# The first batch in halves: q over all partitions in natural head order, swapped weight rows, g on GpSimd's queue, and a new order of the work

## The chip, the cores and the metric

One Trainium2 chip, one of its cores. The time of a kernel is the device time of one execution in microseconds (us). TensorE (PE) multiplies matrices, VectorE (DVE), ScalarE (ACT) and GpSimd (POOL) work on elements, SyncE (SP) starts most transfers. The engines run each its own list of instructions in order and wait for each other through semaphores.

## The reference

Inputs are q, k and v of shape 8 x 8 x 576 x 64 (batch, head, token, element), a vector g of 64, and the weights of four experts.

```python
kv = np.einsum('bhsd,bhse->bhde', k, v)
out = np.einsum('bhsd,bhde->bhse', q, kv)
rms = np.sqrt(np.mean(out * out, axis=-1, keepdims=True) + 1e-06)
x = out / rms * g_norm          # then x as batch x token x 512
...
logits = x @ w_gate             # the two best of four experts, with softmax weights w
for e in range(E):
    q, k, v = x @ wq[e], x @ wk[e], x @ wv[e]
    scores = scale * (q @ k.transpose(0, 2, 1))   # causal
    a = softmax(scores)
    ye = a @ v @ wo[e]
    out += (w where e was chosen) * ye
```

So there are two stages: linear attention without a mask over eight heads with a norm on each head's 64 elements, and a mixture of four causal attention experts with heads of 64 elements.

## The kernel before

All sizes are fixed: eight batches, 576 tokens, which are five blocks of up to 128 (`NB`), and 512 elements, which are four chunks of 128 (`NCH`, two heads each). The work is written as some 1,100 small tasks, each a function in the table `emit`: for example `("kv", b, c)` is the product of k and v of chunk c of batch b. The string `ORDER` lists all tasks by number, `ENGINE` gives each task its engine (S is SP's queue, C ACT's queue, A ACT, V DVE, G POOL), and `SLOTS` gives the buffers and the PSUM banks. The loop at the end issues the tasks in the listed order, so that each engine's own order and each DMA queue's order are written out by hand.

A batch goes through these tasks. `lk` and `lv` load k and v, each in four transfers (four heads by one part of the tokens) that write every second partition. `lq` loads q: the even chunks in one transfer over 128 partitions, the odd chunks in two transfers over 64 neighbouring partitions each, because in odd chunks the two heads stand in swapped order (`head`, line 307). `kv` makes the products in PSUM (line 389), `kvc` copies them to `kvs` and `kvx` moves blocks of 32 partitions to `kvm` (lines 394 to 404). `qc` turns q by 32 x 32 blocks on DVE (line 411). `o` multiplies q with `kvs` and `kvm` (line 424; one task for each pair u of chunks), `oc` copies the result to `ob`, `sq` squares it to `sqs`. `ms` sums the squares of each head by matmuls (line 456). `ln`, `rs`, `na`, `nb` and `lo` make the reciprocal root with one Newton step (lines 472 to 492), on 128 partitions for the whole batch. `bc` spreads the root over a head's elements (line 531) and `xm` multiplies it with `ob` into `xT` (line 538). `G`, `R`, `L` and `lt` make the gate logits in the same way. Then come the projections `qp`, `kp` and `v` (lines 610 and 590), the scores `sc`, `exp` and `msk`, the products `pv`, the turned result `ot`, the output products `y`, and the stores `st`.

The vector g is folded into the weights: `lw` loads a weight matrix in two halves, and `ws` scales its rows by g while it copies them (line 367); `wgs` does this for the gate's weights (line 352). `lgv` and `lwg` load g and the gate's weights on ACT's queue.

`ZEROS` puts matmuls of zeros ahead of some tasks, 61 in all, whose results nobody reads. Each matmul on 32-bit data appears as two passes in the profile.

Loads on SP's queue share eight completion semaphores in turn: a load waits until the one eight places before it has landed.

Of the kernel before, what the change touches and what calls it, by code (L numbers as in the profile page):

```python
# [10 lines left out]
FP32 = mybir.dt.float32  # L11
# [21 lines left out]
    "1d4j6Y3T1V6S3N6W4f1c3S1Z1I1g4h3U4k3Z1-6X1J3O4d4eAX3V3a204i1x4g0P6U2+1D6P1y3W1E3J4l1F3K213g4p1f2-4m6Q6R3X8T4n1e"
    "4r4t1t1h1u3Y6i6T6k3o1i1z3L304s6l4q4o3q3p1j3M1+1k6V224u3r3d4v3b3w6j233c2425398b8Y3fAc4x3s4y3y4z4+3A6Z6a3t6b8c6c"
    "3z4-3x551l6d506h593C8W6g3u566f5B4w0RAa8U3v5A6e1m8Z573h5C518V586m3B6o6n266q6u3P6s3H8X3Q5V0Q5R6r8a6t5X6p5S3D5W5L"
    "8m523I6v8o426w6y3E536x8d6zCY8e415M3e278f6+6-8g5470AbCd5YEb3F76715Z0S778h7C2H3G7D5a3i2E8l8p5u8j2IAd3j8i3kAW725s"
    "3l8n5D7A7B5N5v2FEi78AU5P5t5Q798k5OCZ8r5b8w8yEh5c5d8q5G3-3+5e8s3m738x5f5+8u5g5j7460Cc61405y3n5w758tAn66435-7t44"
    "5xAV7Y8z7uAo457Q7R5lAY5EAq5FAZ65645z7W7S7E8v7Z5T5U8+Ae5H5I90Af9146927X7TAg93Ec94Ah7gAi7e9GCf7hEe9AAp47Ak7O7f9H"
    "2BCh7vAj487P5J2C7w637a9E95Cg9B9C8-5kAlAm4I5i5K7b9D9FEa4J5h5mAsAx4L7F5n5o5pEf964M7x7zEZ62AzAy7k7yCuArAtAv499a9S"
    "A+9b7UAw9Q67Au7+A-9T7H9R689769866A7G98CbB07cB1B25qB37V7m9928CrCsB44A7d7I7j84297M2DB56B7l4F9I4G7N7i9L6C9z4K7J9+"  # L40
    "5r9cBDCt9x9Y4H9dBHBE9J9y9kB6Ca9Z7-B7BI9l9iBB809j9K7K7nBCCe7L9-A37oCiCjCkClEdB87pA481A0CmBF7qCnB9BG8283CqCp9eA1"
    "Co9fA24C4D6D6ECwCvCxD1CyC-D2CzEtEgEjEkElEmD09gA5C+9hEsD387857r8889A9D5D68AEvA6En6M8BEoEq7sBbD7BZ6J6NBc9UBd9MD8"
    "EuByBA9N9WEr6FBeD9BJ6K9nBz9mDAB+9pEpBT9XBR9VBUBfBa9O9q9oB-BSBK4BDJA8DHD4BgDKDFDIDLBlDB8CBm6GDGDMEwBr6H8DEyExEz"
    "E+9PA7Bh9rBLF0BMF29sAABi8NBVF3F18OC2BWBqC0E-9tC3DCF4C6ABC19uC4DD2JCBBjC7ACC5AD8KDhDEBkF6AEBXDNBNAFF7DfF88LBYAG"
    "9vBn8QDi9w8RF9FADgFIFJF5AHDj2GBoFGDnDoFBBOFCFD8H4NFHC8DODZ8EDaDkE0BPBpFE8FFKCCE1FL2ABQAIALDVFMAJAM6IDWFFFNDrE2"
    "DQFiE3FOBs8MFjDpDP8IDRFPCAC9BtDqBuDlDmBvE4CDE5CEFRCFBwCGBxFQDtFgFhDSFc8JEADuEBDvE8E6FdE9EFFSFmE7AODbDcFnARDXDT"
    "DYAPFTANG9G7GAFaAS6OG8DsDdFbCHFoFUGBDeFqCIFrDwDUECFpCSCMEGEEAKEDDxGCFYFWCNDyGFDzFVCTFkFXGD6LFwFuGJFZEHGGEIGLGE"
# [3 lines left out]
ENGINE = (
    "SSSSSSSSSSCCVSVSASASASGSVSASAVVVVVVGGVVVVVVVAAAAAAVAVVAAAVVGVVVVVVVVVVVVVGAVGVVGVVVAVVVVVAVVVAVAVAVAVAGGGGGVVG"
    "VVAVVVAVAVAVAVAGGGGGVVGVVAVASVASVASVASSSSSSSSSSSVVVVAVVGAVVVVVVAAVAAGAGVVAAAVVGVVVGVVVVVVVVVGAGGVVGVVVVVAVAVAV"
    "VVAVAVAVAVAGGGGGVVGVVVVAVAVAVAVAVAGGGGGVVGVVVVASVVSVASVASVASSSSSSSSSSSVVVVVGGGGVVVVVVVGAGAAAGVVAAAVVVVVVVVVVVV"
    "VVVVGAGGVVGVAVAVVVAVAVVVAVAVAVAVAGGGGGVVGVVAVAVAVAVAVAVAGGGGGVVGVVAVVSVASVASVASSSSSSSSSSSVVVVAVVGGVVVVVVAGVAAA"
    "VGVVAAAVVVVVVVVVFVFVVVVGAGGVVGVVVAVVVAVVVVVAVAVAVAVAGGGGGVVGVVAVAVAVAVAVAVAGGGGGVVGVVVVVSVASVASVVSVASSSSSSSSSS"
    "SVVVVAGGGAVVVVVVVGAGAGVGVVAAAVVGVVVGVVVVVVVVVGAGGVVGVAVVVAVVVAVVVAVAVAVAVAGGGGGVVGVVAVAVVVAVAVAVAGGGGGVVGVVVVA"
    "SVASVASVASSSSSSSSSSSVVVVAGGVAVVVVVVVAAAAGVGVVAAAVVGVVVVVVFVVVFVVGAGGVVGVVVVVVVAVAVVVAVAVAVAVAGGGGGVVGVVVVAVAVA"
    "VAVAVAGGGGGVVGVVVVASVASVVSVASVASSSSSSSSSSSVVVVAAVGGVVVVVVVAVGAAAGVVAAAVVGVVVVVVVVVVVVVGAVGVVGVVVVVVVAVAVVVAVAV"
    "AVAVAGGGGGVVGVVVVAVAVAVAVAVAGGGGGVVGVVAVASVASVASVASSSSSSSSSSSVVVVVGGGAVVVVVVAGAAVAAGVVAAAVVGVVVVVVFVFVFVVGAGGV"  # L60
    "VGVVVAVAVVVVVAVVVAVAVAVAGGGGGVVGVVVGVVVVAVVVVVAVAVAVAGGGGGVVGVVVGVVAVAVASVVSVASVASVAS"
)
# [14 lines left out]

def names(nb):
# [36 lines left out]
def kernel(  # L115
# [232 lines left out]

    def lwg():
        queue(("lwg",)).dma_start(wg_in[:], moe_w_gate.rearrange("(n p) e -> p n e", p=P))  # L350
# [481 lines left out]
```

## Time and profile before

| | |
|---|---|
| median of 3 runs | 210.72 us (209.38 to 211.36) |
| the profiled execution | 210.22 us, of which the span from the first to the last instruction is 208.5 us |
| mean granted TensorE clock | 0.993 |
| busy, share of the span | PE 94%, PEld 78%, DVE 59%, ACT 62%, POOL 35% |
| moved by DMA | 40.33 MB, mean 193 GB/s |

PE is the matmul, PEld the load of its weights, which overlaps it. A row of the timeline gives the start in us, the length in us, the engine, the line of the kernel, the operation, what it writes and reads, the count, and in brackets the idle time before it and what ended that. A row of the chain of work gives start, length and what the end of the program waited for at that time. SPq and ACTq are the issue of transfers on the queue of SP and ACT.

### The profile page before, as it was taken

To read this page: it belongs to the slowest core of one execution; us is meant where nothing else is said; L and a number is where in the kernel's file an instruction comes from. 1 tells how busy PE (TensorE), PEld (TensorE's weight loads), DVE (VectorE), ACT (ScalarE), POOL (GpSimd) and SP (SyncE) were. 2 spreads that over 40 slices of the span, in tenths; PEclk is the share of its full clock that TensorE was granted. 3 is DMA by queue.
4 is the path that set the end of the run, shared out by engine and by line. 5 is a ranking of instruction groups with operands and counts; after the bars stand their busy time and mean duration, and the time that the engine had idled before them with its cause. 6 is when DMAs were issued, how large, how long until landed. Compare 5 with 4: busy or idle time off the path is not lost.

```text
span 208.5 us, 7342 instructions
## 1 busy us (share of the span) xinstructions
PE 195.4 (94%) x3066; PEld 163.2 (78%) x3066; DVE 123.3 (59%) x305; ACT 129.6 (62%) x229; POOL 73.7 (35%) x185
## 2 busy tenths in 40 slices
PE   7779879999999999999999999999999999999990
PEld 7768556688988687869886879888976969898970
DVE  7007449457874954977576497474686566734550
ACT  2000722765986765667576677868549955688881
POOL 6001013510793260429162343234707331532510
PEclk9999999999999999999999999999999999999997
DMA  4999995999999993879259806144001010814685
GB/s 111 302 290 284 360 218 143 302 267 217 332 357 348 248 319 140 206 197 371 79 145 252 288 3 202 65 174 135 0 13 43 9 46 0 293 62 183 233 304 195
DMA packets 34385, 40.33 MB, mean 193 GB/s; under 512 B 9008, under 2 KB 25392, under 8 KB 34352
## 3 DMA queue, kind: packets, MB, share of 16 engines
q1 hardware_dynamic: 33520, 39.56, 63.4%
q8 instruction: 24, 0.39, 0.8%
q10 hardware_dynamic: 832, 0.30, 0.7%
q14 instruction: 9, 0.07, 0.1%
HBM read 30.42 MB, written 9.44 MB: 191 GB/s over the span
## 4 chain that ended last, share of the span: by engine, by line
PE 83%; DMA 8%; ACT 4%; DVE 2%; issue 1%; SPq 0%; POOL 0%; ACTq 0%; DVEq 0%; POOLq 0%
PE banks L610 17%; PE banks L590 9%; PE banks L389 9%; PE banks L424 8%; PE banks L640 8%; PE banks L456 8%; PE banks L685 7%; PE banks L758 6%; PE banks L793 3%; PE banks L531 3%; DMA v_b<-in_v_dram 3%; DMA k_b<-in_k_dram 3%; PE banks L728 2%; DMA out_dram<-stage 2%; ACT stage L301 1%; PE banks L514 1%
## 5 line engine op out<-in xcount | busy, mean ns | idle before, releaser
L652 ACT ACTIVATE PT<-banks 128x1024 bf16<-128x1024 f32 (+1 forms) x64 | 51.0, 838 | 11.8 <-PE banks L640 10.4
L659 POOL TENSOR_SCALAR_AFFINE_SELECT PT<-PT 128x256 bf16<-128x256 bf16 (+1 forms) x80 | 29.4, 386 | 15.3 <-ACT PT L652 14.7
L538 DVE TENSOR_TENSOR xT<-banks,ob 128x576 fp32r<-128x576 f32 x32 | 23.5, 748 | 5.6 <-PE banks L531 4.8
L411 DVE STREAM_TRANSPOSE qT<-q_b 128x576 f32<-128x576 f32 x32 | 23.4, 754 | 4.0 <-DMA q_b<-in_q_dram 4.0
L448 POOL TENSOR_TENSOR sqs<-ob 128x576 f32<-128x576 f32 x17 | 19.4, 1146 | 16.0 <-ACT ob L301 15.4
L590 PE MATMUL banks<-wv_r,xT 128*128 128x256 f32 x160 | 24.8, 286 | 0.1
L389 PEld LDWEIGHTS banks<-v_b,k_b 128*64 128x64 f32 x640 | 19.6, 138 | 5.5 <-DMA v_b<-in_v_dram 2.2
L389 PE MATMUL banks<-v_b,k_b 128*64 128x64 f32 x640 | 21.1, 224 | 2.9 <-DMA v_b<-in_v_dram 2.9
L640 PE MATMUL banks<-qTp,kT 64*128 64x192 f32 (+3 forms) x224 | 22.4, 308 | 0.3 <-issue 0.3
L590 PEld LDWEIGHTS banks<-wv_r,xT 128*128 128x128 f32 x160 | 21.1, 189 | 1.1 <-issue 0.5
L640 PEld LDWEIGHTS banks<-qTp,kT 64*128 64x128 f32 x224 | 16.2, 185 | 6.1 <-issue 2.2
L758 PE MATMUL banks<-wo_b,OT 128*128 128x256 bf16 x144 | 20.4, 274 | 0.0
L610 PE MATMUL banks<-xT,wq_r 128*128 128x288 f32 x128 | 20.3, 300 | 0.0
L424 PE MATMUL banks<-qT,kvs 32*64 32x288 f32 x256 | 19.6, 411 | 0.4 <-DVE xT L538 0.3
L793 PE MATMUL banks<-zeros 128*128 128x128 f32 x122 | 16.4, 296 | 3.8 <-DVE root L484 1.2
L610 PE MATMUL banks<-xT,wk_r 128*128 128x288 f32 x128 | 19.7, 298 | 0.0
L793 PEld LDWEIGHTS banks<-zeros 128*128 128x128 f32 x122 | 15.4, 208 | 5.0 <-DVE root L484 1.7
L301 ACT COPY stage<-banks 128x512 f32<-128x512 f32 x30 | 17.2, 594 | 2.9 <-PE banks L758 1.7
L424 PE MATMUL banks<-qT,kvm 32*64 32x288 f32 x256 | 18.2, 411 | 0.3 <-DVE kvm L302 0.3
L402 POOL COPY kvm<-kvs 32x256 f32<-32x256 f32 x19 | 7.6, 398 | 29.8 <-ACT kvs L301 16.2
L301 ACT COPY ob<-banks 128x576 f32<-128x576 f32 x20 | 12.3, 646 | 9.0 <-PE banks L424 9.0
L610 PEld LDWEIGHTS banks<-xT,wq_r 128*128 128x128 f32 x128 | 17.7, 188 | 0.3 <-issue 0.2
(93 smaller groups left out, 312.0 us busy)
## 6 DMA issues: line engine op xcount, KB each, us to landing
out_dram<-stage SPq DMA_DIRECT2D x32, 256.0 KB, 2.9
k_b<-in_k_dram SPq DMA_DIRECT2D x16, 320.0 KB, 6.9
v_b<-in_v_dram SPq DMA_DIRECT2D x16, 320.0 KB, 6.9
q_b<-in_q_dram SPq DMA_DIRECT2D x8, 576.0 KB, 8.2
q_b<-in_q_dram SPq DMA_DIRECT2D x15, 288.0 KB, 7.9
k_b<-in_k_dram SPq DMA_DIRECT2D x16, 256.0 KB, 5.9
v_b<-in_v_dram SPq DMA_DIRECT2D x16, 256.0 KB, 6.0
out_dram<-stage SPq DMA_DIRECT2D x8, 128.0 KB, 2.8
```

Source lines behind the costliest of these rows:

```text
L301: return nc.scalar.copy(dst, src)
L389: use(nc.tensor.matmul(p_kv[hh * Dh : (hh + 1) * Dh, c, :], lhsT=k_t(b)[:, h, j, :], rhs=v_t(b)[:, h, j, :], start=(j == 0), stop=(j == LO ...
L411: nc.vector.transpose(q_part(b, dh)[:, ms].rearrange("p m (t i) -> p m t i", t=RUN), q_t(b)[:, ms, :, dh * 32 : (dh + 1) * 32],)
L424: use(nc.tensor.matmul(bank(n)[at : at + Dh, 0:HALF], lhsT=(kvs if z == dh else kvm)[b % 2][pp, m], rhs=q_part(b, dh)[pp, m], start=(dh == ...
L538: use(nc.vector.tensor_tensor(out=at_half(xTs[b % 2], u, z), in0=both(ns)[:, :, 0:HALF], in1=ob[:, u::2, z * HALF : (z + 1) * HALF], op=Al ...
L590: use(nc.tensor.matmul(bank(n)[:, 0 : E * Hd], lhsT=blocks_of(xTs[b % 2], c)[:, i * P : (i + 1) * P], rhs=w_r["v"][:, c, :, :].rearrange(" ...
L610: use(nc.tensor.matmul(bank(ns[s])[:, 0:HALF], lhsT=w_r[nm][:, c, 2 * pr : 2 * pr + 2, :].rearrange("p e f -> p (e f)"), rhs=blocks_of(xTs ...
L640: use(nc.tensor.matmul(bank(ns[el])[:, o : o + hi - lo], lhsT=kTs[(2 * b + pr) % 3][pp, kb * P : (kb + 1) * P], rhs=tiles["qTp", b, pr][pp ...
L652: use(nc.scalar.activation(PTs[(2 * b + pr) % 3][:, :, 512 * j : 512 * j + o], both(ns)[:, :, 0:o], ACTF.Exp, scale=scale), *ns)
L659: nc.gpsimd.affine_select(out=d, in_=d, compare_op=AluOpType.is_ge, fill=0.0, base=0, pattern=[[0, 2], [1, w]], channel_multiplier=-1,)
L758: use(nc.tensor.matmul(bank(n)[:, cols], lhsT=OT[:, pr, at : at + P], rhs=wo_b[:, pr, cols], start=(pr == 0), stop=(pr == EP - 1), skip_gr ...
L793: use(nc.tensor.matmul(bank(at)[:, 2 * P : 3 * P], lhsT=zeros[:, 0:P], rhs=zeros[:], start=True, stop=True, skip_group_check=True), at)
```

## The change

The heads stand in natural order in every chunk, so that one load brings a pair of chunks over all 128 partitions. Odd chunks of `xT` now hold their two heads the other way round than before, which the weights make up for: `ws` swaps the two groups of 64 rows of odd chunks while it scales, in three instructions instead of one, and `wgs` does the same. g and the gate's weights are loaded by GpSimd's queue. Batch 0 goes in two halves (chunks 0 and 1, chunks 2 and 3) from `kv` to `xT`: each half has its own PSUM bank, its own copies and moves, its own sums, and its own root on 64 partitions. `ZEROS` holds 48 matmuls instead of 61. `ORDER`, `ENGINE` and `SLOTS` are new for the whole program; batch 0 now starts with heads 4 to 7.

```diff
 ZEROS = {
-    ("kv", 0, 0): 28, ("kv", 0, 2): 4, ("o", 0, 1): 17, ("ms", 0): 6, ("bc", 0, 0, 0): 6,
+    ("kv", 0, 2): 31, ("kv", 0, 0): 14, ("o", 0, 0): 3,
 }
...
+def halves_of(b):
+    return ((0,), (1,)) if b == 0 else ((),)
...
     def head(hh, c):
-        return 2 * c + (hh ^ (c % 2))
+        return 2 * c + hh
...
-    def lq(b, odd):
-        eng = nc.scalar if b == 0 else nc.sync
-        if not odd:
-            nc.sync.dma_start(
-                q_t(b)[:, ::2].rearrange("i m t d -> i m (t d)"),
-                q[b].rearrange("(m k a) (i t) d -> k (a i) m (t d)", k=2, a=2, t=RUN)[0],
-            )
-            return
-        for a in range(2):
-            (eng if a else nc.sync).dma_start(
-                q_t(b)[a * Dh : (a + 1) * Dh, 1::2].rearrange("i m t d -> i m (t d)"),
-                q[b, head(a, 1) :: 4].rearrange("m (i t) d -> i m (t d)", t=RUN),
-            )
+    def lq(b, u):
+        nc.sync.dma_start(
+            q_t(b)[:, 2 * u : 2 * u + 2].rearrange("i m t d -> i m (t d)"),
+            q[b, 4 * u : 4 * u + 4].rearrange("(m a) (i t) d -> (a i) m (t d)", a=2, t=RUN),
+        )
 
     def lgv():
         for h in range(2):
-            queue(("lgv",)).dma_start(g_part[h * Dh : (h + 1) * Dh], g_norm.unsqueeze(1))
+            nc.gpsimd.dma_start(g_part[h * Dh : (h + 1) * Dh], g_norm.unsqueeze(1))
 
     def lwg():
-        queue(("lwg",)).dma_start(wg_in[:], moe_w_gate.rearrange("(n p) e -> p n e", p=P))
+        nc.gpsimd.dma_start(wg_in[:], moe_w_gate.rearrange("(n p) e -> p n e", p=P))
+
+    def parts():
+        yield slice(0, P), slice(0, P), 0
+        for h in range(2):
+            yield slice(h * Dh, (h + 1) * Dh), slice((1 - h) * Dh, (2 - h) * Dh), 1
...
     def ws(nm, p):
...
-        if engine["ws", nm, p] == "A":
-            nc.scalar.mul(out, src, g_part[:, 0:1])
-        else:
-            ew(("ws", nm, p)).tensor_scalar_mul(out=out, in0=src, scalar1=g_part[:, 0:1])
+        for to, pp, odd in parts():
+            d, x, g = out[to, :, odd::2], src[pp, :, odd::2], g_part[pp, 0:1]
+            if engine["ws", nm, p] == "A":
+                nc.scalar.mul(d, x, g)
+            else:
+                ew(("ws", nm, p)).tensor_scalar_mul(out=d, in0=x, scalar1=g)
...
+    def kv_bank(b, c):
+        return small("kv", b, c // 2) if b == 0 else small("kv", b)
+
+    def chunks(h):
+        return slice(2 * h[0], 2 * h[0] + 2) if h else slice(0, NCH)
+
+    def rows_of(h):
+        return slice(h[0] * Dh, (h[0] + 1) * Dh) if h else slice(0, P)
...
-    def kv_copy(b):
-        (n,) = small("kv", b)
-        use(copy(("kvc", b), kvs[b % 2][:].rearrange("p c d -> p (c d)"), bank(n)[:, 0 : NCH * Dh]), n)
+    def kv_copy(b, *h):
+        (n,) = kv_bank(b, chunks(h).start)
+        p_kv = bank(n)[:, 0 : NCH * Dh].rearrange("p (c d) -> p c d", c=NCH)
+        use(copy(("kvc", b) + h, kvs[b % 2][:, chunks(h)], p_kv[:, chunks(h)]), n)
...
-    def ln(b):
-        ms, n = part_sums(b)
-        use(nc.scalar.activation(root[:], ms, ACTF.Ln, bias=eps[:, 0:1], scale=1.0 / Dh), n)
+    def ln(b, *h):
+        ms, n = part_sums(b, h)
+        pp = rows_of(h)
+        use(nc.scalar.activation(root[pp], ms, ACTF.Ln, bias=eps[pp, 0:1], scale=1.0 / Dh), n)
...
     def xm(b, u, z):
         ns = big("bc", b, u, z)
+        cs, cols = slice(2 * u, 2 * u + 2) if b == 0 else slice(u, NCH, 2), slice(z * HALF, (z + 1) * HALF)
         use(nc.vector.tensor_tensor(
-            out=at_half(xTs[b % 2], u, z), in0=both(ns)[:, :, 0:HALF], in1=ob[:, u::2, z * HALF : (z + 1) * HALF],
-            op=AluOpType.mult,
+            out=xTs[b % 2][:, 0 : NCH * S].rearrange("p (n s) -> p n s", s=S)[:, cs, cols],
+            in0=both(ns)[:, :, 0:HALF], in1=ob[:, cs, cols], op=AluOpType.mult,
         ), *ns)
```

The start of the new order, as the engines' lists have it (later tasks are left out):

```
SP    lk 0 heads 4-7 part 0, lv 4-7 part 1, lk 4-7 part 1, lv 0-3 part 1, lv 4-7 part 0, lk 0-3 part 0,
      lq 0 chunks 2-3, lv 0-3 part 0, lk 0-3 part 1, lq 0 chunks 0-1, eight loads of k and v of batch 1,
      lq 1 chunks 0-1, lw k 0, lq 1 chunks 2-3, lw q 0, lw k 1, lv 2, lw v 1, lw v 0, lv 2, lw q 1, ...
PE    31 zeros, kv 0 2, kv 0 3, 14 zeros, kv 0 0, kv 0 1, o 0 1, 3 zeros, o 0 0, ms 0 (second half), ms 0 (first half),
      kv 1 0, kv 1 1, bc 0 1 0, bc 0 1 1, kv 1 2, kv 1 3, G 0, bc 0 0 0, bc 0 0 1, o 1 0, lt 0, kp 0 0, o 1 1, qp 0 0, kp 0 1, ...
DVE   qc 0 1 0, wgs, kvx (half 1), qc 0 1 1, qc 0 0 1, qc 0 0 0, oc 0 1 0, oc 0 0 0, nb and lo of half 1 and nb of half 0,
      xm 0 1 0, lo of half 0, xm 0 1 1, qc 1 0 1, qc 1 0 0, L 0, xm 0 0 1, xm 0 0 0, qc 1 1 0, qc 1 1 1, kpc 0 0, ws k 1, ...
```

More of the change, by code (lines that the diff above doesn't have):

```diff
@@ L33 @@
[L33 to L47, printed above, removed]
@@ L55 @@
[L55 to L59, printed above, removed]
@@ L528, in spread_mm @@
         for r in range(2):
-            pp = slice(0, P) if engine["bc", b, u, z] == "F" else slice(r * Dh, (r + 1) * Dh)
-            at = 8 * r + 4 * z + 2 * u
+            half, odd = (u, r) if b == 0 else (r, u)
+            pp = slice(0, P) if engine["bc", b, u, z] == "F" else slice(half * Dh, (half + 1) * Dh)
+            at = 8 * half + 4 * z + 2 * odd
             use(nc.tensor.matmul(
@@ L786, in zero_matmuls @@
         if n[0] in ("kv", "v", "y", "ot", "lt", "ms", "G"):
-            at = small(*(n[:2] if n[0] == "kv" else n))[0]
+            at = (kv_bank(*n[1:]) if n[0] == "kv" else small(*n))[0]
         elif n[0] == "o":
```

113 lines of the change are left out of this document (68 added, 45 removed).

## Prediction

> **What bounds the kernel now.** I read the page first, then the busy time of each engine by stretches, then the timeline and the chain of work of the first 45 us, then the DMA rates of the same stretches.
>
> ```profile
> span 208.5 us, 7342 instructions
> ...
> PE 195.4 (94%) x3066; PEld 163.2 (78%) x3066; DVE 123.3 (59%) x305; ACT 129.6 (62%) x229; POOL 73.7 (35%) x185
> ```
>
> ```profile
> 40.00:60.00 20.00, 19.91 (x311) 16.71 (x304) 14.19 (x32) 13.78 (x24) 7.82 (x21) 1.00 1.04 286
> 40.00:200.00 160.00, 159.28 (x2550) 133.54 (x2543) 102.75 (x246) 114.34 (x201) 64.14 (x160) 1.00 0.58 177
> ```
>
> The columns of the stretches are length, then PE, PEld, DVE, ACT and POOL busy, granted clock, DMA share, GB/s. From 40 to 200 us PE is busy for 159.28 of 160 us at a granted clock of 1.00. Its matmuls after the start are the same in both kernels (four `kv`, two `o`, four projections and so on for each batch), so the end of the program moves with the time at which PE stops waiting. That is decided in the first 38 us. Here are PE's rows there (start, length, engine, line; some from the timeline, three from the chain of work):
>
> ```profile
> 1.11 7.94 PE L793 MATMUL banks<-zeros 128*128 128x128 f32 x56 [1.11 <-DVE zeros L197]
> 11.07 1.39 PE L389 MATMUL banks<-v_b,k_b 128*64 128x64 f32 x40 [2.01 <-DMA v_b<-in_v_dram]
> ...
> 14.40 1.39 PE L389 MATMUL banks<-v_b,k_b 128*64 128x64 f32 x40 [0.86 <-DMA v_b<-in_v_dram]
> 16.30 4.06 PE L793 MATMUL banks<-zeros 128*128 128x128 f32 x34 [0.52 <-DVE kvs L302]
> 20.36 1.24 PE banks L424 x32
> ...
> 24.95 1.18 PE L456 MATMUL banks<-sqs,ones 128*32 128x288 f32 x16
> ...
> 30.30 1.39 PE L389 MATMUL banks<-v_b,k_b 128*64 128x64 f32 x40
> ...
> 35.26 2.25 PE banks L424 x62
> 37.51 2.31 PE banks L610 x16
> ...
> 43.08 1.06 PE banks L610 x8
> ```
>
> The rows of `zeros` are filling that nobody reads. What PE waits for in between stands on the other engines:
>
> ```profile
> 15.82 0.42 DVE L302 COPY kvs<-banks 128x256 f32<-128x256 f32 x1 [10.48 <-PE banks L389]
> ...
> 18.30 2.76 DVE L411 STREAM_TRANSPOSE qT<-q_b 128x576 f32<-128x576 f32 x4 [1.32 <-DMA q_b<-in_q_dram]
> ...
> 22.69 1.76 ACT L444 ACTIVATE sqs<-banks 128x576 f32<-128x576 f32 x3
> 24.30 1.23 ACT L301 COPY ob<-banks 128x576 f32<-128x576 f32 x2
> 26.22 0.50 ACT L474 ACTIVATE root<-banks,eps 128x288 f32<-128x288 f32 x1 [0.70 <-PE banks L456]
> 26.75 0.44 ACT L477 ACTIVATE hi<-root 128x288 fp32r<-128x288 f32 x1
> 27.23 0.53 ACT L480 ACTIVATE root<-hi,low 128x288 f32<-128x288 f32 x1
> 27.80 0.46 DVE L484 SCALAR_TENSOR_TENSOR root<-banks,root 128x288 f32<-128x288 f32 x1 [3.24 <-ACT root L480]
> 28.29 0.52 DVE L489 SCALAR_TENSOR_TENSOR lo<-root,low,hi 128x288 fp32r<-128x288 f32 x1
> ...
> 32.78 1.41 DVE L538 TENSOR_TENSOR xT<-banks,ob 128x576 fp32r<-128x576 f32 x2
> ...
> 35.51 0.72 DVE L538 TENSOR_TENSOR xT<-banks,ob 128x576 fp32r<-128x576 f32 x1
> ```
>
> So the ramp is one chain: k and v of all heads (14.40), `kvs` and `kvm`, q (18.30), `o` (20.36), squares, the chain of small operations on the root (26.22 to 28.81), and the products into `xT`, the last of which ends at 36.23. The projections start at 37.51. Under it lie the loads:
>
> ```profile
> 2.50:7.00 4.50, 4.50 (x36) 4.50 (x35) 2.84 (x15) 0.00 (x0) 1.63 (x10) 1.00 0.89 239
> 8.00:12.00 4.00, 1.99 (x42) 1.80 (x42) 0.00 (x0) 0.00 (x0) 0.00 (x0) 1.00 1.09 348
> 12.00:17.00 5.00, 3.62 (x70) 3.25 (x67) 1.10 (x3) 0.00 (x0) 0.65 (x2) 1.00 1.06 253
> 20.00:22.00 2.00, 2.00 (x60) 1.48 (x66) 1.05 (x2) 0.37 (x1) 0.00 (x0) 1.00 1.06 376
> ...
> 26.50:31.00 4.50, 3.29 (x51) 2.47 (x45) 2.25 (x4) 1.20 (x3) 0.79 (x1) 1.00 1.04 212
> ```
>
> The DMA engines are full from 8 us on, but at different rates: k and v give 348 GB/s, 12 to 17 us with the q loads that write 64 neighbouring partitions 253, 20 to 22 us with the even chunks of batch 1's q over 128 partitions 376, and the weights in 256-byte pieces 212.
>
> **The change, part by part.**
>
> *Loads.* `lq` becomes two DMAs over 128 partitions, each with the two chunks that one `qc` pair reads; before, each pair needed all three loads. Nothing runs on the ACT queue at the start. SP's order is new: the four loads of heads 4 to 7 are among the first five (0.26 MB or 0.33 MB each), q of these heads is seventh, the rest of k and v ends with the ninth, q of heads 0 to 3 is tenth. Summed in that order: 1.51, 2.36, 2.95 and 3.54 MB, batch 1's k and v at 5.90, its first q half at 6.49, the first weights at 6.75, its second q half at 7.34. I take 239 GB/s from 2.5 to 5 us, 350 for k, v and q after that, 212 for weights, and 0.6 us from the last bytes to the semaphore: about 8.4, 10.8, 12.5, 14.2, 21.0, 22.6, 24.0 and 25.8 us. The slow bound is 239 until 7 us and 300 after: 9.1, 11.9, 13.9, 15.9, 23.7, 25.7, 27.2 and 28.9.
>
> *PE up to `o`.* Zeros: 62 passes, 7.94 us and six more at 4.06 / 34 = 0.12, end at 9.8, where the data of heads 4 to 7 is there by either bound. `kv` 0,2 and 0,3 take 1.39, to 11.2; 28 passes of zeros take 3.3, to 14.5; `kv` 0,0 and 0,1 end at 15.9; `o` 0,1 takes 1.24 (17.1), six passes 0.7 (17.8), `o` 0,0 ends at 19.0; before, the first `o` of the pair started at 20.36. Beside it, hidden: `qc` of the first half (two of 0.69) from 10.8, `kvs` and `kvm` of each half right behind their matmuls. That doubles the small copies (two and eight for one and four), but the first set has until 15.9, and the second is one copy and two moves on each of ACT and POOL, 0.4 each by the rows below, done by 17.1.
>
> ```profile
> 33.38 0.37 ACT L301 COPY kvs<-banks 128x256 f32<-128x256 f32 x1 [5.62 <-PE banks L389]
> 33.78 0.40 ACT L301 COPY kvm<-kvs 32x256 f32<-32x256 f32 x1
> ```
>
> *Halves to `xT`.* On ACT the square, the copy and the square of the first half (0.6 each) end by 19.0, the two squares of the second by 20.3. The sums of the second half take half of 1.18 and end at 20.9. The root chain now runs twice on 64 partitions; its rows have 288 elements on each partition either way, so I price each as before: ACT 1.47 and 1.47 to 23.2, DVE gives the first `lo` at 22.7 and the second, behind one product, at 24.9. That extra 2.4 us on ACT and DVE lies beside `kv` of batch 1 (2 x 1.39 from 20.9, broken by the first `bc`, some 0.5 after `lo` at 22.7), the gate matmuls (1.18 again, behind the last copy of `ob` on ACT, 23.8) and the second `bc`, to 26.3. DVE then goes product (25.7), two `qc` (27.1), `weigh` (about 0.4), two products, 28.9 against 36.23. PE does `o` 1,0 meanwhile.
>
> *To the projections.* `kp` 0,0 at 28.9 to 30.0; `o` 1,1 behind two `qc` (30.4) to 31.6; `qp` 0,0 to 32.7 and `kp` 0,1 to 33.7, at 1.06 each. By then PE has done one projection more than before at 39.82, so the same point of before is 40.88: a gain of 7.1 us. With the slow bound only `kv` 1,2 is late, by 0.5, so 6.6.
>
> *Weights and g.* Each `ws` becomes three instructions. The rows:
>
> ```profile
> 34.21 0.72 ACT L371 ACTIVATE wk_r<-stage,g_part 128x512 fp32r<-128x512 f32 x1
> ...
> 36.22 0.47 DVE L373 TENSOR_SCALAR wq_r<-stage,g_part 128x512 fp32r<-128x512 f32 x1
> ```
>
> Three of half size cost between 1.0 and 1.2 on ACT (0.36 by elements, 0.40 by the move above) and 0.7 to 1.2 on DVE; I take 1.1 and 0.9. `ws` k,0 lies in ACT's gap before `o` 1,0 ends; the one to watch is `ws` k,1 on DVE, from 31.1 to 32.0, needed at 32.7. Cost zero, at the bound 0 as well. `g` and `wg` go from ACT's queue to GpSimd's. The trace of before has no such queue; the nearest row is ACT's:
>
> ```profile
> 2.75 0.61 ACTq L350 DMA_DIRECT2D wg_in<-in_moe_w_gate_dram  x1
> ...
> DMA to landing us min/median/max: 6.6/6.6/6.6
> ...
> 3.54 0.65 POOL L281 MEMSET vext<- 64x260 bf16 x2
> ...
> 5.12 0.21 DVE L257 CAST ident_b<-ident_f 128x128 bf16<-128x128 f32 x1
> ```
>
> The second line is the landing time of that load, the last two are the end of POOL's and of DVE's fills. POOL is free at 4.2, so at 6.6 us g and `wg` land at about 11. DVE's `wgs` waits for them, with `kvx` 0,0, the second `qc` and all else of DVE queued behind it, 1.9 us of work before `o` 0,1 may start. So 13.9 is early enough, 9.7 us after the issue: cost zero. If that cover is gone, each further us is one us. [...]
>
> *Later batches.* PE's order is new for all 160 us. Of their idle time I count 0.7 us in the old order; I take 1.6 in the new one, an estimate with bounds 0 and 4, as PE asks for batch 4's k and v sooner (first rival). DVE gets some copies of ACT; both stay under 70% of the span.
>
> *The end.* Only the last store changes its queue.
>
> ```profile
> 204.36 1.11 SPq L773 DMA_DIRECT2D out_dram<-stage  x2
> ```
>
> Zero; between -0.3 and +0.6, one issue of the pair.
>
> **Sum.** 210.22 (the profiled execution, 1.72 beside its span) - 7.1 + 0.9 = 204.0. That execution is 0.50 below the median of the runs; I leave the sum as it is.
>
> **The rivals.**
>
> 1. *The DMA engines give part of it back.* Batch 4's `kv` stood here before:
>
> ```profile
> 81.40 2.48 PE banks L389 x80
> ```
>
> The new list puts it ahead of about 11.4 us of matmuls that stood before it (both `o`, the sums and the gates of batch 3, two projections of batch 2 and some smaller ones, by the rows above), so PE wants it at 81.4 - 7.1 - 11.4 = 62.9. Its last load ends at 18.1 MB of the new list. At 31 us, when SP stands at a weight load whose buffer ACT frees behind `o` 1,0 (28.3 and three operations, 30.7), 8.9 MB are in; the other 9.2 MB take 26 us at 350 GB/s, 5 us early. For it: 286 GB/s from 40 to 60 us before. Against it: that stretch held q loads of 64 partitions. At 270, 9.2 MB take 34 us, PE waits 2.7, and the time is 206.7.
> 2. *The supply is the bound, and it is slower than before.* The same place at the rate of the weights, 212 GB/s: 9.2 MB take 43.4, PE waits about 12 us, the time is 216. It decides from about 245 GB/s down, where the wait is the 6.2 that the sum gains. For it: 253 with q among the loads. Against it: only q by halves shows such rates, and those are gone.
> 3. *g is late, so the ramp gains nothing.* Landing at 20 instead of 11 puts `o` 0,1 at 21.9, and all behind it 6 us later: 210. Against it: 6.6 us on ACT's queue with the same traffic.
>
> **How the numbers follow.** The forecast, a gain of 4.5 to 8, has 0.62; rival 1 (206 to 208.5) 0.17; rival 3 and other ways to no change 0.07; rival 2, with any wait of a new order that costs over 8 us, 0.14. Faster by over 1% (about what a measurement here can tell) is the forecast and rival 1, 0.79; within 1% 0.07; slower 0.14. The low end is the ramp's 7.1, no new idle time and 0.8 for the unpriced parts, 202.3; the high end is rival 1 at its worst, 208.8.
>
> **What would show it.** Right: `kv` starts at about 9.8, released by the zeros; `o` 0,1 at about 16; the first projection near 29; q loads at 350 GB/s; PE idle under 2 us from 40 us on. Wrong: `wgs` waiting for g after 14 us; PE waits on k or v near 45 to 65 us; a granted clock below 1.00 in the ramp, where fewer zeros are run.

## The result, and the profile after

The changed kernel took 204.26 us (median of four runs, 203.79 to 204.58) beside 210.2 for the kernel before (209.38 to 211.36): a ratio of 0.972 with a 95% interval of 0.969 to 0.975. The forecast was 204.0. (Three executions in the experiments below took over 1.5% longer than the fastest of the same kernel and are left out of the medians.) Its profiled execution took 203.79, with this span and busy time (the page of the changed kernel):

```profile
span 202.0 us, 7288 instructions
...
PE 193.4 (96%) x3040; PEld 160.1 (79%) x3040; DVE 134.6 (67%) x329; ACT 128.1 (63%) x229; POOL 71.8 (36%) x186
```

TensorE's first 36 us, from the timeline and the chain of work of the changed kernel (start, length; `L812` is the zeros, `L400` kv, `L436` o, `L468` the sums and gates, `L629` the projections):

```profile
1.14 9.02 PE L812 MATMUL banks<-zeros 128*128 128x128 f32 x62 [1.14 <-DVE zeros L203]
10.09 1.39 PE L400 MATMUL banks<-v_b,k_b 128*64 128x64 f32 x40
11.40 3.39 PE L812 MATMUL banks<-zeros 128*128 128x128 f32 x28
14.72 1.39 PE L400 MATMUL banks<-v_b,k_b 128*64 128x64 f32 x40
16.11 1.16 PE banks L436 x32
...
18.13 1.26 PE banks L436 x32
19.22 2.56 PE L468 MATMUL banks<-sqs,ones 128*32 128x288 f32 x16
21.71 1.39 PE L400 MATMUL banks<-v_b,k_b 128*64 128x64 f32 x40
...
29.25 1.28 PE banks L629 x8
...
31.69 2.31 PE banks L629 x16
33.99 2.08 PE banks L468 x32
```

No row carries a wait for data: kv follows the zeros and o follows kv. The first o starts at 16.11 instead of 20.36, the first projection at 29.25 instead of 37.51. At 33.99 TensorE has done what it would have done at 40.88 before, by the prediction's reckoning (two projections by 39.82, and one of 1.06 more). Beside it, VectorE and ScalarE of the same timeline:

```profile
12.71 0.78 DVE L423 STREAM_TRANSPOSE qT<-q_b 128x576 f32<-128x576 f32 x1 [7.05 <-DMA q_b<-in_q_dram]
13.41 0.91 DVE L357 TENSOR_SCALAR wgs<-wg_in,g_part 64x8 f32<-64x8 f32 x4
...
15.89 1.44 DVE L423 STREAM_TRANSPOSE qT<-q_b 128x576 f32<-128x576 f32 x2 [0.55 <-DMA q_b<-in_q_dram]
...
22.65 0.52 DVE L506 SCALAR_TENSOR_TENSOR lo<-root,low,hi 64x288 fp32r<-64x288 f32 x1
...
24.76 0.50 DVE L506 SCALAR_TENSOR_TENSOR lo<-root,low,hi 64x288 fp32r<-64x288 f32 x1
...
27.55 1.40 DVE L557 TENSOR_TENSOR xT<-banks,ob 128x576 fp32r<-128x576 f32 x2
...
31.24 1.09 DVE L375 TENSOR_SCALAR wk_r<-stage,g_part 128x256 fp32r<-128x256 f32 x3
...
26.47 1.56 ACT L373 ACTIVATE wk_r<-stage,g_part 128x256 fp32r<-128x256 f32 x3 [0.28 <-DMA stage<-in_moe_wk_dram]
```

The last product into `xT` ends at 28.95 (before 36.23). `wgs` has no wait in brackets: g was there. The load rates in the stretches that the prediction showed, and TensorE's busy time behind the ramp (changed kernel; columns as there: length, PE, PEld, DVE, ACT, POOL, granted clock, DMA share, GB/s):

```profile
2.50:7.00 4.50, 4.50 (x32) 4.50 (x31) 3.15 (x15) 0.00 (x0) 3.54 (x13) 1.00 0.95 283
8.00:12.00 4.00, 4.00 (x65) 3.81 (x64) 0.00 (x0) 0.45 (x2) 0.00 (x0) 1.00 0.91 310
12.00:17.00 5.00, 5.00 (x98) 4.44 (x96) 3.67 (x9) 1.49 (x6) 0.46 (x2) 1.00 1.07 381
40.00:60.00 20.00, 19.68 (x354) 16.31 (x356) 14.62 (x33) 14.77 (x25) 7.91 (x18) 1.00 1.05 359
60.00:80.00 20.00, 19.06 (x358) 14.90 (x352) 16.29 (x41) 13.45 (x26) 9.62 (x23) 1.00 0.93 323
100.00:120.00 20.00, 19.19 (x279) 14.57 (x279) 15.06 (x37) 11.46 (x23) 9.67 (x23) 1.00 0.65 219
40.00:191.00 151.00, 148.77 (x2436) 124.45 (x2437) 104.88 (x247) 102.87 (x179) 60.55 (x154) 1.00 0.52 176
```

From 12 to 17 us, where q is among the loads, the rate is 381 GB/s instead of 253. From 40 us on TensorE idles 2.23 us instead of 0.72, and the list of its waits names most of it, two gaps inside the weighted sums (`L704`) that nothing in the profile releases:

```profile
PE banks L704 <- issue: 1.6, 2, 0.8
```

So of the lead of 6.9 us at the projections 6.1 are left at the last matmul of y, which ends at 197.31 against 203.37; the program ends 4.7 us behind that instead of 5.1, which adds 0.4.

### The profile page after: what moved, and what is told of

Its sections match the earlier page's. It is cut to its first block, busy times and chain, and to the rows that moved or that the text cites. A ratio compares the mean times of both kernels' runs of the same rounds, so it can differ in the third digit from the quotient of the medians.

```text
span 202.0 us, 7288 instructions
## 1 busy us (share of the span) xinstructions
PE 193.4 (96%) x3040; PEld 160.1 (79%) x3040; DVE 134.6 (67%) x329; ACT 128.1 (63%) x229; POOL 71.8 (36%) x186
## 4 chain that ended last, share of the span: by engine, by line
PE 88%; DVE 4%; ACT 3%; issue 2%; POOL 0%; DVEq 0%; POOLq 0%
PE banks L629 17%; PE banks L609 9%; PE banks L436 9%; PE banks L659 9%; PE banks L400 9%; PE banks L704 8%; PE banks L468 8%; PE banks L777 7%; PE banks L812 7%; PE banks L747 3%; PE banks L549 3%; PE banks L531 1%; ACT stage L304 1%; DVE osc L732 1%; DVE xT L557 1%
## 5 line engine op out<-in xcount | busy, mean ns | idle before, releaser
L671 ACT ACTIVATE PT<-banks 128x1024 bf16<-128x1024 f32 (+1 forms) x64 | 51.3, 838 | 10.8 <-PE banks L659 10.0
L678 POOL TENSOR_SCALAR_AFFINE_SELECT PT<-PT 128x256 bf16<-128x256 bf16 (+1 forms) x80 | 28.8, 380 | 21.6 <-ACT PT L671 21.3
L609 PE MATMUL banks<-wv_r,xT 128*128 128x256 f32 x160 | 24.1, 287 | 0.0
L659 PE MATMUL banks<-qTp,kT 64*128 64x320 f32 (+3 forms) x224 | 21.8, 309 | 0.4 <-DVE ob L305 0.3
L609 PEld LDWEIGHTS banks<-wv_r,xT 128*128 128x128 f32 x160 | 20.6, 188 | 1.1 <-DVE wv_r L375 0.7
L400 PEld LDWEIGHTS banks<-v_b,k_b 128*64 128x64 f32 x640 | 19.6, 138 | 2.2 <-issue 1.3
L400 PE MATMUL banks<-v_b,k_b 128*64 128x64 f32 x640 | 21.1, 224 | 0.0
L659 PEld LDWEIGHTS banks<-qTp,kT 64*128 64x128 f32 x224 | 15.7, 185 | 5.9 <-issue 1.5
L629 PE MATMUL banks<-xT,wq_r 128*128 128x288 f32 x128 | 20.3, 302 | 0.0
L629 PE MATMUL banks<-xT,wk_r 128*128 128x288 f32 x128 | 19.7, 297 | 0.0
L436 PE MATMUL banks<-qT,kvs 32*64 32x288 f32 x256 | 19.5, 411 | 0.2 <-DVE qT L423 0.2
L704 PEld LDWEIGHTS <-PT 128*128 128x128 bf16 x480 | 15.9, 97 | 4.6 <-issue 1.8
L704 PE MATMUL banks<-vext,PT 128*128 128x65 bf16 x480 | 17.7, 193 | 1.7 <-issue 1.6
L436 PE MATMUL banks<-qT,kvm 32*64 32x288 f32 x256 | 18.6, 410 | 0.0
L629 PEld LDWEIGHTS banks<-xT,wq_r 128*128 128x128 f32 x128 | 17.5, 188 | 0.8 <-issue 0.4
L629 PEld LDWEIGHTS banks<-xT,wk_r 128*128 128x128 f32 x128 | 17.6, 188 | 0.1
L304 ACT COPY ob<-banks 128x576 f32<-128x576 f32 x17 | 10.6, 638 | 9.3 <-PE banks L436 8.2
L305 DVE COPY ob<-banks 128x576 f32<-128x576 f32 x15 | 11.3, 751 | 7.6 <-PE banks L436 4.2
```

Of the source, the lines that this page charges most:

```text
L400: use(nc.tensor.matmul(p_kv[hh * Dh : (hh + 1) * Dh, c, :], lhsT=k_t(b)[:, h, j, :], rhs=v_t(b)[:, h, j, :], start=(j == 0), stop=(j == LO ...
L436: use(nc.tensor.matmul(bank(n)[at : at + Dh, 0:HALF], lhsT=(kvs if z == dh else kvm)[b % 2][pp, m], rhs=q_part(b, dh)[pp, m], start=(dh == ...
L609: use(nc.tensor.matmul(bank(n)[:, 0 : E * Hd], lhsT=blocks_of(xTs[b % 2], c)[:, i * P : (i + 1) * P], rhs=w_r["v"][:, c, :, :].rearrange(" ...
L629: use(nc.tensor.matmul(bank(ns[s])[:, 0:HALF], lhsT=w_r[nm][:, c, 2 * pr : 2 * pr + 2, :].rearrange("p e f -> p (e f)"), rhs=blocks_of(xTs ...
L659: use(nc.tensor.matmul(bank(ns[el])[:, o : o + hi - lo], lhsT=kTs[(2 * b + pr) % 3][pp, kb * P : (kb + 1) * P], rhs=tiles["qTp", b, pr][pp ...
L671: use(nc.scalar.activation(PTs[(2 * b + pr) % 3][:, :, 512 * j : 512 * j + o], both(ns)[:, :, 0:o], ACTF.Exp, scale=scale), *ns)
```

## The experiments

Times are medians beside the kernel before on the same chip, with the ratio to it and its 95% interval. "First projection" is its start in the profiled execution, 29.25 us in the changed kernel.

### Control

The changed kernel again: 205.12 us, 0.9745 (0.970 to 0.979).

> The changed kernel once more, unaltered, as the control of this group. Theory: the 2.2 us that TensorE lies idle from 40 us on, against 0.7 us in the kernel before, belong to the new order of the instructions, so the two gaps of 0.8 us inside the weighted sums at about 69 and 110 us come back at the same places; time 204.3 us within 0.5. Rival: the gaps are an accident of that one execution; then they lie elsewhere or are gone, and the profiled execution is up to 1.5 us shorter.

The execution that was profiled took 207.5 us beside 204.35 to 205.42 of the others, so its rows are not compared, and this run doesn't decide between theory and rival. The median lies 0.3 us above the theory's range: runs of this kernel spread more than I had thought. The gaps can be followed in the other runs: with g on ScalarE's queue both come back at the same places (1.9 us in all), with q in more transfers they sum to 0.8. So they are no accident, but no fixed part of the order either; the later experiments show what they are.

### q in 64 neighbouring partitions

```diff
-        nc.sync.dma_start(q_t(b)[:, 2*u : 2*u+2] ..., q[b, 4*u : 4*u+4] ...)      # 128 partitions
+        for a in range(2):
+            nc.sync.dma_start(q_t(b)[a*Dh : (a+1)*Dh, 2*u : 2*u+2] ..., q[b, 4*u+a : 4*u+4 : 2] ...)
```

> Only the shape of the q transfers is undone: each pair of chunks comes in two transfers of 64 neighbouring partitions, in the same order and on the same queue. Theory (a transfer that spans all 128 partitions is what lifts q from some 230 to some 370 GB/s): 0.59 MB per pair take 2.5 us instead of 1.6, so the second q pair of batch 0 lands 1.8 us later (17.7 instead of 15.9 us) and the first weights, three pairs down the queue, 2.7 us later (29.1 instead of 26.4). The first projection had 1.2 us between the end of its weights' scaling and its start, so it moves by 1.5 to 2.7 us: 205.8 to 207.3 us. Rival (the rate follows the number and size of transfers, not the partitions they span): as the run with two transfers of 128 partitions, whatever that gives.

221.74 us, 1.053 (1.048 to 1.058): the direction of the theory, at six to twelve times its price (17.5 us above the changed kernel for 1.5 to 3.0).

### q in as many transfers, each over 128 partitions

```diff
+        for m in range(2*u, 2*u+2):
+            nc.sync.dma_start(q_t(b)[:, m] ..., q[b, 2*m : 2*m+2] ...)
```

> The control for number and size: each pair of chunks comes in two transfers as well, but each of one chunk over all 128 partitions. Theory: q still runs at about 370 GB/s, the landings stay within 0.4 us, time 204.3 us within 0.4. Rival (more and smaller transfers are the price): as slow as the run with 64 partitions, 1.5 us or more above the changed kernel.

204.67 us, 0.972 (0.969 to 0.976): as the changed kernel. The stretches of both, first those with 64 partitions, then the one with 128:

```profile
10.00:20.00 10.00, 7.83 (x146) 6.81 (x145) 2.56 (x7) 2.27 (x8) 0.57 (x2) 1.00 1.07 236
40.00:60.00 20.00, 17.87 (x212) 15.42 (x211) 14.47 (x37) 10.50 (x20) 2.47 (x8) 0.83 1.07 273
```

```profile
10.00:20.00 10.00, 10.00 (x189) 8.55 (x187) 4.76 (x10) 3.69 (x10) 0.57 (x2) 1.00 1.03 359
```

The DMA engines are as busy (1.07 and 1.03) and move 236 GB/s instead of 359. So the number and size of transfers cost nothing here, and the span over partitions is the whole difference; why 64 partitions are slower the two runs don't show.

My price was wrong because I counted 0.9 us for each of three slow pairs and nothing else. The other loads were held up too: the first weights landed at 32.7 us, where 29.1 was expected and the changed kernel has 26.4. The first projection came at 34.6 us, 5.3 late instead of 1.5 to 2.7, and the rest was lost later: from 40 to 60 us TensorE is busy 17.87 of 20 us at a granted clock of 0.83, and its waits with 64 partitions begin with

```profile
PE banks L705 <- issue: 4.3, 3, 2.2
PE banks L401 <- DMA k_b<-in_k_dram: 4.2, 3, 2.1
```

The supply can't follow the new order, as in the second rival of the prediction, and that rival's 216 us was nearer than my expectation of this run. But the mechanism is not its one long wait for k and v. Those waits come to 4.7 us in the whole run, and the gaps inside the weighted sums (`L705`, taken up below) to 4.3. And two stops, of 2.1 us until 51.6 and of 2.2 us until 127.9, are followed by a fall of the granted clock to 0.50, from 53.0 to 59.8 and from 128.1 to 131.5 us. Eight projection matmuls take 2.12 us there instead of 1.06, so 10.2 us at half the clock are, by an estimate from these numbers, some 5 us of the loss. The kernel before had the slow transfers in half of its q only and was not starved by them (0.09 us idle from 40 to 60 us).

### g and the gate weights on ScalarE's queue

```diff
-        nc.gpsimd.dma_start(g_part ...);  nc.gpsimd.dma_start(wg_in ...)
+        nc.scalar.dma_start(g_part ...);  nc.scalar.dma_start(wg_in ...)
```

> Only the queue of g and the gate weights is undone: they are issued by ScalarE's queue as before. Theory: those loads were hidden in both places; the first k and v may land up to 0.5 us earlier, since the rate dips to 210 to 235 KB per us at 6 to 8 and 10 us while the other queue's packets run, but the first kv matmuls stand behind zeros until 10.1 us and cannot use it: 204.3 us within 0.4, kv at 10.1 us again. Rival 1 (moving them was part of the gain): 1 us or more slower. Rival 2 (the software queue costs the ramp): 0.5 us or more faster.

205.03 us, 0.9754 (0.970 to 0.981): 0.3 us above the theory's range, but 0.1 us from the control, from which it can't be told; neither rival occurred. q of heads 0 to 3 landed at 14.9 instead of 15.9 us and the first weights at 24.9 instead of 26.4, but kv stood behind its zeros until 10.7. That the loads were hidden in both places held; whether the earlier landings are worth anything waits for a kernel with fewer zeros (below).

### No zeros

```diff
-    ("kv", 0, 2): 31, ("kv", 0, 0): 14, ("o", 0, 0): 3,
```

> The changed kernel without its zero matmuls ahead of kv and o of batch 0. Theory 1 (the zeros keep TensorE's clock up): in the runs so far one zero matmul took 0.213 us at first and 0.111 us from a moment between 4.2 and 7.1 us on; without them that switch comes only after the first real work, so kv of batch 0 starts earlier (8.9 us, at the landing of its v) but takes 2.8 us instead of 1.4, o and the sums twice as long as well, first projection 2 to 4 us later: 206 to 208.5 us. Theory 2 (they are mere filler, and now too long): kv starts 1.2 us earlier and nothing is lost: 203.2 to 204.0 us.

205.74 us, 0.980 (0.976 to 0.985); the first projection at 31.0. That is 0.3 us below the range of the first theory and far from the second's. The timeline without zeros shows kv at the landing of its v, taking 2.40 us for the same 40 matmuls that later take 1.39:

```profile
9.02 2.40 PE L400 MATMUL banks<-v_b,k_b 128*64 128x64 f32 x40 [9.02 <-DMA v_b<-in_v_dram]
14.74 2.40 PE L400 MATMUL banks<-v_b,k_b 128*64 128x64 f32 x40 [3.32 <-DMA k_b<-in_k_dram]
...
23.34 1.39 PE L400 MATMUL banks<-v_b,k_b 128*64 128x64 f32 x40
```

So the zeros do work: they bring TensorE to full speed. But there are too many: kv of heads 4 to 7 could have started at 9.0.

### Batch 0 not in halves

```diff
 def halves_of(b):
-    return ((0,), (1,)) if b == 0 else ((),)
+    return ((),)
```

(with one copy, one root and one `lo` for batch 0; the first `bc` and product stand behind that `lo`)

> Only the halves of batch 0 are undone: kv is copied once after all four chunks, the sums, the root and lo are made once for all 128 rows; loads, queues, zeros and the rest of the order stay. Theory (halves are a small part of the gain): o waits for kvs and kvm of all chunks (1.3 us after kv instead of at once), the norm chain starts after both o, so the first projection comes 1.4 to 3 us later: 205.6 to 207.3 us. Rival 1 (the halves are most of the gain): 4 us or more, 208 us and above. Rival 2 (the first projection waits for its weights, which land at 26.4 us, not for x): less than 0.5 us.

207.62 us, 0.988 (0.984 to 0.992): 2.5 us above the control and 3.4 above the first measurement. Its chain of work:

```profile
17.18 2.07 PE banks L430 x32
20.11 1.26 PE banks L430 x32
...
32.09 1.30 PE banks L623 x8
```

o waits for all heads (17.18), the first projection starts at 32.09, 2.8 us late: inside the 1.4 to 3 of the theory, though the time lies 0.3 above its range. Rival 2 falls: the first projection waited for x, not for its weights. Of the whole gain of 5.9 us the halves are 2.5 to 3.4 by the times and 2.8 by the first projection: about half, and not the small part that the theory supposed. (The gaps without a releaser are 2.0 us here, 0.4 more than in the changed kernel.)

### The kernel before with the new q transfers

```diff
 # kernel before, its own ORDER, ENGINE, SLOTS and ZEROS
-    q in 3 transfers, two of them over 64 partitions
+    q in 2 transfers over 128 partitions, natural heads, weights' rows swapped
```

(batch 0's transfer on ACT's queue is one of the three, so all of q now comes by SP's queue)

> The kernel before, with its own order, zeros and queues and batch 0 whole, but with the new q transfers over 128 partitions (so in natural head order, with the swapped weights). Theory (the ramp follows the loads, the order only takes what they give): the waits of 2.0 and 0.9 us before the kv matmuls of batch 0 shrink to 0.5 to 1.5 us in all, o of batch 0 starts at 18 to 19.5 us instead of 20.3, the weights land some 2 us earlier: 207.5 to 209.5 us. Rival 1 (without the new order faster loads give nothing): 210 us or more. Rival 2 (the loads alone are the whole gain): 204 to 205.5 us.

208.68 us, 0.994 (0.991 to 0.997).

```diff
-    ("kv", 0, 0): 28, ("kv", 0, 2): 4, ("o", 0, 1): 17, ...
+    ("kv", 0, 0): 28, ("kv", 0, 2): 4, ("o", 0, 1): 5, ...
```

> As the run before this one, with the zeros ahead of the first o of batch 0 cut from 17 to 5. Theory: in the kernel before 34 zero matmuls ran from 16.3 to 20.4 us, though kvm was ready at 17.0; with q there, o starts as soon as kvm is, at 17 to 18 us, and all behind it comes 1 to 2.5 us earlier than with 17: 206 to 208 us. Rival (q or batch 1's k and v come no earlier than the zeros end): as the run with 17 zeros, within 0.4 us.

206.81 us, 0.986 (0.983 to 0.989). The chain of work of the first and then of the second:

```profile
17.38 1.24 PE banks L430 x32
...
34.31 2.37 PE banks L623 x16
```

```profile
15.70 1.31 PE banks L430 x32
...
32.70 2.36 PE banks L623 x16
```

Both times fall in the theory's ranges; o starts even earlier than it said (17.4 and 15.7). With whole transfers in the old order the projections start 3.2 us earlier than 37.51, and 4.8 with the shorter filler. The spans, 206.5 and 204.9 us, are only 2.0 and 3.6 shorter than 208.5, so 1.2 is given back in each. By the times the loads alone are worth 1.5 us, with zeros cut to fit them 3.4; the rest of the 5.9, about 2.5, came only with the halves and the new order. The halves alone account for that much by the experiment above; no run has them in the old order, so the two are not told apart.

### Loads of later batches left out

```diff
     def load(m, dst, src, b, p, z):
+        if b >= 3: return                  # lq likewise, on the buffers of batches 0 and 2
```

> The loads of q, k and v of batches 3 to 7 are left out (those batches compute on what the earlier ones left in the buffers); TensorE's instructions and their order are unchanged. Theory (the gaps inside the weighted sums are TensorE waiting for its next 16 KB of instructions, whose transfer stands behind data packets; it ended 1.2 to 1.6 us after that transfer in every run so far): without data traffic at 60 to 115 us the gaps of 0.8 to 1.6 us at about 70 and 110 us are gone or under 0.4 us, TensorE is busy at least 19.7 of 20 us at 60 to 80 and 19.8 at 100 to 120; 202.5 to 203.8 us. Rival (the gaps belong to the order of the instructions, or to a unit that comes late): they stay at 0.8 us or more, 204.3 us or more.

202.8 us, 0.965 (0.960 to 0.971). The same stretches as above, with hardly any traffic:

```profile
60.00:80.00 20.00, 19.68 (x354) 15.28 (x350) 17.30 (x43) 13.24 (x25) 9.70 (x23) 1.00 0.01 2
100.00:120.00 20.00, 19.96 (x286) 15.44 (x285) 15.88 (x36) 11.02 (x22) 9.65 (x23) 1.00 0.10 35
```

19.68 and 19.96 instead of 19.06 and 19.19: both gaps are gone (0.02 us of the first stretch short of the expected 19.7). The DMA view of a small window shows the transfer in question, one packet of 16 KB on the instruction queue. In the changed kernel it lies between 67.2 and 68.4 us (first fence; the gap ends at 69.81), without the loads between 64.5 and 66.0 (second):

```profile
q1 hardware_dynamic: 230, 0.35, 88.0%
q8 instruction: 1, 0.02, 4.9%
```

```profile
q8 instruction: 1, 0.02, 3.9%
```

TensorE's list is the same in both and its start differs by 0.24 us, but the packet runs 2.5 us later among data packets (67.3 against 64.8 by its record), and the second gap's at 108.4 instead of 104.5, about 1 us of which is what TensorE lags by then. In every profile that has gaps of over 0.4 us inside the weighted sums, each of them ended 1.2 to 1.6 us behind the end of such a packet.

### The same filler in fewer instructions

```diff
-            ... rhs=zeros[:]                     # 31 times 128 columns ahead of the first kv
+            ... rhs=zeros[:, 0:w]                # 15 times 128 and 8 times 256
```

> The changed kernel with the filler as long as it was but made of fewer instructions: ahead of the first kv 15 zeros of 128 columns and 8 of 256 stand for the 31 of 128, so TensorE's instruction stream is shorter by the same 8 calls as in the run with fewer zeros, and nothing else moves. Theory (the gaps at 70 and 110 us depend on which instruction a 16 KB block of the stream ends at): the ramp is that of the changed kernel (kv at 10.1 to 11.1 us, first projection at 29.2 to 30.2 us), the gaps sum to at most 0.6 us instead of 1.6 to 2.9, as in the run with fewer zeros; 203.2 to 204.4 us. Rival (the gaps shrank there because everything came 1 to 2 us earlier): they sum to 1.5 us or more, 204.3 us or more.

203.49 us, 0.970 (0.965 to 0.974). kv at 10.29, first projection at 29.45, as in the changed kernel, and its waits:

```profile
PE banks L704 <- issue: 0.2, 1, 0.2
```

Eight calls fewer in the list, at times within 0.2 us of the changed kernel's, took 1.4 us of gaps away. The time alone doesn't show it, since the intervals overlap: the last matmul of y ends 0.8 us earlier (196.5 for 197.3), but the end behind it took 0.7 us longer in this execution. The gaps do show it, against the rival. So it matters which instruction the 16 KB blocks end at. I read it so: with fewer instructions ahead, a block reaches further into the work, and the transfer may come later; that TensorE needs the next block just there isn't recorded.

### Fewer zeros

```diff
-    ("kv", 0, 2): 31, ("kv", 0, 0): 14, ("o", 0, 0): 3,
+    ("kv", 0, 2): 24, ("kv", 0, 0): 14, ("o", 0, 0): 2,
```

> The changed kernel with fewer zeros: 24 instead of 31 ahead of the first kv, 2 instead of 3 ahead of the second o. Theory (31 zeros end at 10.1 to 11.1 us, by when TensorE's clock doubles, but v of heads 4 to 7 is there at 8.9 us): kv starts at 8.9 to 9.5 us, the second kv when its k lands at about 14.3 us, the second o when its turned q is there at 17.4 us instead of 18.1 to 19.0; first projection at 28.4 to 28.9 us, limited by the scaling of its weights, which ends at 28.0: 0.4 to 1.5 us below the changed kernel, 203.0 to 204.2 us. Rival (the wait after the shorter filler lets the clock fall): kv or o take twice as long, as without zeros, 205 us or more.

203.18 us, 0.967 (0.962 to 0.971).

```diff
+    ("kv", 0, 2): 24, ("kv", 0, 0): 12, ("o", 0, 0): 2,     # and g, wg on ScalarE's queue
```

> The same with g and the gate weights issued by ScalarE's queue, as in the kernel before, and 12 zeros ahead of the second kv. Theory: from the third q transfer on all loads land 0.9 to 1.5 us earlier than with GpSimd's queue (second k of heads 0 to 3 at 13.4 instead of 14.3 us, the first weights at 24.9 instead of 26.4 us), and with fewer zeros TensorE can now use it: second o at 16.5 us, first projection at 27.3 to 28 us, 1.0 to 2.5 us below the changed kernel: 202.0 to 203.5 us. Rival (the loads behind the first stage don't set the first projection): as the run with fewer zeros alone, within 0.4 us.

202.35 us, 0.962 (0.957 to 0.967): the best of all, some 1% below the changed kernel. Its timeline, and two rows of its chain:

```profile
9.05 1.39 PE L400 MATMUL banks<-v_b,k_b 128*64 128x64 f32 x40 [0.28 <-DMA k_b<-in_k_dram]
...
14.84 1.16 PE banks L436 x32
...
27.77 1.28 PE banks L629 x8
```

kv now waits for its data and runs at full speed; the first projection comes at 27.8 (28.6 with g on GpSimd's queue and 14 zeros). Both times lie in the theory's ranges; with 24 zeros alone kv came at 9.7 instead of 8.9 to 9.5, behind its v. What the theory did not say is that the eight or ten calls fewer also shift the 16 KB blocks: the gaps sum to 0.4 us and to none. By the run with the same filler in fewer instructions that is up to 1.4 us of profiled time, so in the one with 24 zeros alone the shift may be the larger part of the gain; the first projection moved by only 0.6. Against that run the best kernel is 1.1 us faster by medians (203.49 and 202.35), with intervals that overlap.

Nor do the two runs show what the queue of g is worth. Of the 0.85 us between their first projections 0.63 stand already at the first kv, whose v landed at 9.5 us in the one and 8.9 in the other; with g on GpSimd's queue the same load landed anywhere from 8.9 to 10.0 us in other profiles. The remaining 0.2 us are the two zeros fewer.

## Why the prediction was right, point by point

- *The ramp decides.* Right: 6.9 us of lead measured at the point for which 7.1 was worked out. The start of kv (10.1 for 9.8), the first o (16.1 for 15.9), the second (18.1 for 17.8), the two `lo` (23.2 and 25.3 at their ends for 22.7 and 24.9), the last product (28.95 for 28.9) and the first projection (29.25 for 28.9) each lie within 0.5 us. That kv came so near is partly luck: the zeros were priced as in the profile of the kernel before, and the same 62 passes ended between 9.9 and 11.1 us in the profiles of this case (last section).
- *The loads.* Mis-sized. They came near the slow bound, not at the forecast: q of heads 4 to 7 at 12.7 us (10.8 forecast, 11.9 slow), k and v of batch 0 at 14.3 (12.5, 13.9), q of heads 0 to 3 at 15.9 (14.2, 15.9), the first weights at 26.4 (24.0, 27.2). The failed step is 350 GB/s from 5 us on; 283 and 310 were measured up to 12 us. By its own rates the fast list comes out 0.2 to 0.4 us earlier than it is written, and no run shows its 0.6 us from the last bytes to the semaphore: where a transfer of SP's queue was the only one under way, its last packet ended 0.33 to 0.47 us before it landed, in the traces of both kernels. The miss cost nothing because the zeros were as long as the late loads, as the prediction had reckoned for its slow bound.
- *g on GpSimd's queue, cost zero.* The two parts of g landed at 11.2 and 11.9 us, beside the 11 worked out from a row; 13.4, when it was used, was late enough. What the step overlooked is the other side: with that queue the loads behind it come later. q of heads 0 to 3 landed at 15.4 to 16.2 us in the seven profiles with this queue and the same q transfers, at 14.7 and 14.9 in the two with ScalarE's; the first weights at 25.2 to 26.4 against 24.9. In the changed kernel this is hidden behind the zeros; that it costs time once they are cut is not shown.
- *Halves.* The chain of small operations on 64 partitions ran at its old prices, as reckoned (0.50, 0.45 and 0.53 us on ScalarE in the chain of work).
- *`ws` in three instructions.* Too low: 1.56 us on ScalarE for 1.1 and 1.09 on VectorE for 0.9. The first ended at 28.0 ahead of its use at 29.25, so it stayed off the path.
- *Later batches, 0.9.* Right in size, not in reason. I thought of transfers that TensorE would ask for sooner; it never waited for one (the kernel with slow q shows that this danger was real). What it idled for, by the inference of the last section, were its own instructions, 1.6 us in the changed kernel. That the size fits is luck.
- *The end, 0.* It gained 0.4, where the bound allowed 0.3; in the other profiles of the new order the end took from 4.7 to 5.4 us, so this belongs to the one execution.
- With the measured terms the sum is 210.22 - 6.9 + 0.8 - 0.4 = 203.7, against 203.79 of the profiled execution. None of the three rivals occurred: no wait for k or v from 45 to 65 us, no wait for g.

## What to carry to other kernels

Judge a transfer by the partitions it spans before its size, and read the rate in the stretch where it runs: with q in the same number of transfers and the DMA engines about as busy, the loads ran at 236 (64 partitions) or at 359 GB/s (128), and the slow ones held up the weights behind them by 6.3 us. When loads come earlier, cut the filler that was counted for the old ones, and set the count by the earliest time at which data can be there: a fixed filler hides a gain as well as a loss. When a new order shows idle gaps that no semaphore explains, look whether an instruction block came late among data packets (here by 2.3 and 2.8 us, at two gaps of 0.8 us) before blaming the order.

## What the runs showed of the hardware that I had not expected

*TensorE's start.* One pass of a zero matmul of 128 x 128 takes 0.213 us at first and 0.111 from some moment on. The granted clock of these rows reads 1.00 throughout, but the trace has its first record of the clock only at that moment (5.0 us in the changed kernel, 7.1 with q in four transfers, 19.9 without zeros), so the 1.00 before it says nothing. Counted in stretches of 2 us of the changed kernel and of the one with q in four transfers (PE busy, count, clock, DMA share, GB/s), with about 11 a stretch at half speed and 20 at full:

```profile
2.00:4.00 2.00, 2.00 (x11) 1.00 0.71 207
4.00:6.00 2.00, 2.00 (x16) 1.00 1.02 321
6.00:8.00 2.00, 2.00 (x21) 1.00 0.90 222
```

```profile
2.00:4.00 2.00, 2.00 (x11) 1.00 0.72 203
4.00:6.00 2.00, 2.00 (x12) 1.00 1.00 316
6.00:8.00 2.00, 2.00 (x15) 1.00 0.92 252
```

The switch came 2.9 to 5.9 us behind the first matmul in the profiles with zeros ahead of the first kv, so a filler of 62 passes ended between 9.9 and 11.1 us; without zeros it came 10.9 us behind the first kv, with 3.3 us of waiting in between. Where only the zeros hold kv back, as in the changed kernel, this goes straight into the time.

*Instruction transfers.* Instructions come in 16 KB packets, which the profile counts on the same 16 DMA engines as the data, 24 in a run (0.39 MB on the instruction queue). They are TensorE's: the run without zeros, whose list differs in TensorE's alone (2944 matmul passes instead of 3040, and as many weight loads fewer), has 23 of them, and in both runs one comes for every 253 to 256 of TensorE's instructions. Behind full queues (a DMA share of 0.99 from 66 to 68 us and of 1.02 from 108 to 110) two came some 2.3 and 2.8 us later than without loads, TensorE's own lag taken off, and TensorE stopped for 0.8 us each time. That such a gap ends 1.2 to 1.6 us behind the packet, and vanishes without the traffic or with another length of the list ahead, is shown; that TensorE stood still for want of just that block is inferred from it.
